# Four lists of rows per place, wide products first, and the odd groups' sums in the first four places: one change to a kernel of Fourier mixing and routed experts

## The chip, the cores and the metric

The kernel runs on one core of a Trainium2 chip. The metric is the device time of one execution in microseconds. Before the change it is 681.73 us, the median of three runs (681.48 to 681.78).

## The reference

2048 tokens of 512 numbers are normalised. Two things are added to them: a Fourier mixing, with the transform written as matrix products over the 512 columns and over the 2048 tokens, and a layer of eight experts, of which each token uses the one with the highest logit.

```python
def _A_ref(x, dft_seq_re, dft_seq_im, dft_hid_re, dft_hid_im):
    a = jnp.einsum("bsd,ed->bse", x, dft_hid_re)
    b = jnp.einsum("bsd,ed->bse", x, dft_hid_im)
    return jnp.einsum("ts,bse->bte", dft_seq_re, a) - jnp.einsum("ts,bse->bte", dft_seq_im, b)

def _B_ref(x, w_gate, w1, w2):          # S, D, F, E = 2048, 512, 1376, 8; K = 1
    logits = xf @ w_gate
    topk_idx = jnp.argsort(-logits, axis=-1)[:, :K]
    ...
    for e in range(E):
        mask = (topk_idx == e)
        w = (gates * mask).sum(-1, keepdims=True)
        h = _silu(xf @ w1[e]) @ w2[e]
        out = out + w * h

xn = _layernorm(x, axis=-1)
return x + _A_ref(xn, ...) + _B_ref(xn, ...)
```

## The kernel before

Every operand of a large product is held as a pair, a high part that ScalarE casts and a low part that VectorE subtracts (`split`, L126 and L127), and each product is three matmuls: high by high, high by low, low by high.

The work runs in this order. First the norms, and a product of the Fourier part with the sequence matrix (L412). Then its "even" groups (L598 to L600), beside which the gate's logits are counted, each expert's tokens are ranked, and every token's row is scattered to its place in a DRAM buffer. Then the experts. Then the "odd" groups of the Fourier part (again L598 to L600), and at last the product with the hidden matrices (L1228 to L1230), to which each token's expert row is added.

The experts are sorted by their number of tokens and each gets a *place*, the fullest first. The place's number of rows is fixed in the program. `SIZES` holds lists of eight such numbers; the program has an arm for each list, written out in full by `finish` (L1041), and a switch takes the first list that holds all the experts' counts. The table `less` holds the lists on the chip but the last; `set_apart` makes a spare tile of `APART` columns ahead of the experts' tiles.

A place is a `Window`. Its rows are loaded turned by a transposing DMA, joined to 32-bit numbers and split into a pair (`turns`), the tile `wth` (in the code `xx`). Then for each of 11 blocks of the hidden width (ten of 128, one of 96): `up` multiplies the place's rows by four chunks of the first weight matrix, silu follows on ScalarE, the result is split into `hh` (L930) and `hl` (L931), and two blocks later `down` multiplies it by the second weight matrix. The weights stream in through SyncE's queue, and their pairs are made three blocks ahead.

The two kinds of place differ in what stands still. With more than 256 rows, the weights are the stationary operand in both products and the moving one has as many columns as the place has rows: 12 matmuls up (L914 to L916) and 12 down (L954 to L956) for each block. With 256 rows or fewer (`twin`), the low part of the rows lies right behind the high part, so that one up matmul of twice the width multiplies both by the weights' high part (wide, 512 columns), and a narrow one multiplies the high part by the weights' low part; both are L911, and wide and narrow alternate over the four chunks, the last two swapped. The halves of the wide result are added by ScalarE and VectorE (L921, L922). Down, the rows are the stationary operand and the moving one has 512 columns: six matmuls (L946 to L948).

Beside the places, VectorE prepares the tokens' sums that the odd groups need, for one of eight token blocks in each place: at block 2 `odd_parts` adds the pair up (L515) and makes three sums (L518, L519), at block 5 `parts` casts and splits these (L498 on ScalarE, L499 on VectorE). All engines' instructions are put in order by a scheduler from the code's order and its own costs, save those that are pinned by `keep_in_program_order` and all of SyncE's.

Of the kernel before, what the change touches and what calls it, by code (L numbers as in the profile page):

```python
# [23 lines left out]
NB = NT // 2  # L24
KD = D // P
# [4 lines left out]
LAG = 2  # L30
RAWS = 4
PAIRS = 4
APART = 104
SHIFT = 56
WARM = 25
DH = D // 2
# [3 lines left out]

SIZES = [[300, 284, 276, 264, 256, 256, 256, 256],
         [310, 290, 278, 272, 266, 256, 256, 256],
         [328, 304, 288, 280, 270, 256, 256, 256]]
WS = SIZES[-1]
XW = 256
WCUM = [sum(WS[:i]) for i in range(E + 1)]
NX = max((S - sum(WS[:m]) + m * (XW - 1)) // XW for m in range(1, E + 1) if sum(WS[:m]) + m <= S)
assert min(map(min, SIZES)) > P and max(WS) <= 3 * P  # L50
assert all(a <= b for s in SIZES for a, b in zip(s, WS))


@with_exitstack
def fnet_moe(ctx, tc, x, cr, ci, dr, di, wg, w1, w1r, w2, w2r, out):
    nc = tc.nc
    V, A, T, G, SY = nc.vector, nc.scalar, nc.tensor, nc.gpsimd, nc.sync
# [11 lines left out]
    def bank(name):  # L69
        if free:  # L70
            return free.pop(0)
        return psum.tile([P, 512], F32, tag="bank", name=name)
# [242 lines left out]
    with tc.high_priority(), tc.manual_schedule(engines={V.engine, A.engine}):  # L315
# [11 lines left out]
        n = norms[1]  # L327
# [22 lines left out]
        n = norms[2]  # L350
# [34 lines left out]
    for i in range(E):  # L385
        G.memset(wsz[:, i:i + 1], float(WS[i]))
        G.memset(wcm[:, i:i + 1], float(WCUM[i]))
    less = cst.tile([P, len(SIZES) - 1, E], F32, name="less")
    for n, sizes in enumerate(SIZES[:-1]):
        for i in range(E):  # L390
# [106 lines left out]
    def parts(b, dst, src):  # L497
        copy = A.copy(xh[b].rearrange("p j d -> p (j d)")[:, dst], src)  # L498
        V.tensor_sub(xl[b].rearrange("p j d -> p (j d)")[:, dst], src,  # L499
                     xh[b].rearrange("p j d -> p (j d)")[:, dst].bitcast(F32))  # L500
        return copy
# [10 lines left out]
    def odd_parts(b):  # L512

        r = others.take()
        tc.keep_in_program_order(V.tensor_add(r, *(v[b].rearrange("p j d -> p (j d)").bitcast(F32) for v in (xh, xl))))  # L515
        t = sums.take()
        t2 = r[:, DH:2 * DH]
        V.tensor_add(t[:, DH:2 * DH], r[:, :DH], t2)  # L518
        V.tensor_add(*(v[:, 2 * DH:].rearrange("p (h d) -> p h d", h=2) for v in (t, r)),  # L519
                     t2[:, None, :].to_broadcast([P, 2, DH]))  # L520
        return r, t
# [131 lines left out]
    def sm(name, shape, dt=F32):  # L653
        return late[0].tile([P] + shape, dt, name=name)
# [57 lines left out]
    def route(cnt):  # L712
# [28 lines left out]
        def by_place(name, v, dst=None):  # L741
            m = sm("m" + name, [E, E])
            r = sm("r" + name, [E]) if dst is None else dst
            V.tensor_mul(m, q, v[:, None, :].to_broadcast([P, E, E]))
            V.reduce_sum(r, m, axis=AX.X)
            return r
# [15 lines left out]
        by_place("snu", num, over)  # L762
        n = len(SIZES) - 1
        past, most, no = sm("past", [n, E]), sm("most", [n]), sm("no", [n])
# [95 lines left out]
    def set_apart(pool):  # L860
        apart = pool.tile([P, APART], F32, name="apart", bufs=1)
        G.memset(apart, 0.0)

    class Window:
# [36 lines left out]
        def up(self, f):  # L901
            m, w = FT[f], self.w
            hi, lo = self.block(0, f // 2, 3)
            t = bank("up")
            for k in range(KD):
                c = (f % 2) * 512 + k * m
                h, l = (self.xx[:, k, a:a + w] for a in (self.at_h, self.at_l))
                if self.twin:
                    work = [(hi, self.xx[:, k, :2 * w], 2 * w), (lo, h, w)]
                    for a, b, n in work if k < KD - 1 else work[::-1]:  # L910
                        T.matmul(t[:m, :n], a[:, c:c + m], b, start=(k == 0 and a is hi),  # L911
                                 stop=(k == KD - 1 and a is hi))
                    continue
                T.matmul(t[:m, :w], hi[:, c:c + m], h, start=(k == 0), stop=False)  # L914
                T.matmul(t[:m, :w], hi[:, c:c + m], l, start=False, stop=False)  # L915
                T.matmul(t[:m, :w], lo[:, c:c + m], h, start=False, stop=(k == KD - 1))  # L916
            if f % 2 or f == NF - 1:
                self.release(0, f // 2)
            s = self.pool.tile([P, self.most], F32, name="sil")
            if self.twin:  # L920
                A.copy(s[:m, :w], t[:m, w:2 * w])  # L921
                V.tensor_add(s[:m, :w], t[:m, :w], s[:m, :w])  # L922
                A.activation(s[:m, :w], s[:m, :w], AF.Silu)
            else:
                A.activation(s[:m, :w], t[:m, :w], AF.Silu)
            free.append(t)
            hh = self.pool.tile([P, self.most], F32R, name="hh", bufs=3)
            hl = self.pool.tile([P, self.most], F32R, name="hl", bufs=3)
            hh, hl = (v[:, self.at_h:self.at_h + w] for v in (hh, hl))
            (A.copy if self.twin and f % 2 else V.tensor_copy)(hh[:m], s[:m, :w])  # L930
            V.tensor_sub(hl[:m], s[:m, :w], hh[:m].bitcast(F32))  # L931
            self.pend.append((f, hh, hl))
# [108 lines left out]
    def finish(sizes, last):  # L1041
# [45 lines left out]
        for i, w in enumerate(wins):  # L1087
            for f in range(NF):
                w.up(f)
                todo.append(w)  # L1090
                if len(todo) > LAG:
                    todo.pop(0).down()
                if f == 2:
                    halves3 = odd_parts(i)
                if f == 5:
                    tc.keep_in_program_order(parts(i, slice(DH, 4 * DH), halves3[1][:, DH:]))
                    others.give(halves3[0])
                    sums.give(halves3[1])
                if i == 0 and f == 8:
                    more.append(mo.enter_context(tc.tile_pool(name="more", bufs=1)))  # L1100
                if i + 1 < E:
                    if f in (3, 4):
                        wins[i + 1].load(f - 3)
                    if f in (6, 8):
                        wins[i + 1].turns(f - 6)
                if i > 0:
                    w0 = wins[i - 1]
                    if w0.twin and f in (2, 3):
                        w0.back(f - 2)
                    if not w0.twin and 6 <= f < 9:  # L1110
                        w0.turn(f - 6)
                    if not w0.twin and f == 10:
                        w0.store()
# [135 lines left out]
        with tc.If(more_windows[0] > 0):  # L1249
            with tc.tile_pool(name="zeros", bufs=1) as zp:  # L1250
                zero = zp.tile([P, 2 * D], U16, name="zero")
                G.memset(zero, 0)
                n = NX * XW // P
                A.dma_start(hx[:n * P, :].rearrange("(n p) d -> p n d", p=P), zero[:, None, :].to_broadcast([P, n, 2 * D]))
                A.dma_start(hx[n * P:, :], zero[:1, :])
            with tc.For_i(0, more_windows[0]) as j, tc.tile_pool(name="further", bufs=1) as fp, \
# [7 lines left out]
                def block(k, b, ahead):  # L1264
                    if (k, b) not in got:
# [3 lines left out]
                w = Window(XW, lambda r, n: xs[bass.ds(xov + r, n), :],  # L1269
                           lambda r, n: hx[bass.ds(j * XW + r, n), :], block, fp)  # L1270
# [27 lines left out]
    for n in tc.Switch(which[0], len(SIZES), hint="sizes"):  # L1298
        finish(SIZES[n], n == len(SIZES) - 1)
# [44 lines left out]
```

## Time and profile before

| | us |
|---|---|
| median of the runs | 681.73 |
| the profiled execution | 681.63 |
| its span, first to last instruction | 679.9 |
| TensorE's matmuls busy | 673.6 |
| VectorE busy | 532.1 |
| ScalarE busy | 407.7 |
| GpSimd busy | 46.3 |

In the rows of the profile, PE is TensorE's matmuls and PEld its weight loads, DVE is VectorE, ACT ScalarE, POOL GpSimd, SP SyncE; a q behind a name is that engine's DMA queue. A row of the timeline has the start, the duration, the engine, the line, the operation, what is written and what is read, the shape (for a matmul rows and columns of the array, then the moving operand), and in brackets how long the engine was idle before and what ended that. Ends of matmuls are modelled, starts are recorded. The experts' places lie between 230.8 and 490 us: those of more than 256 rows, 300, 284, 276 and 264, begin at 230.8, 264.0, 298.7 and 332.2 us, the four of 256 fill the time from 364.1 us on.

### The profile page before, as it was taken

To read this page: it belongs to the slowest core of one execution; us is meant where nothing else is said; L and a number is where in the kernel's file an instruction comes from. 1 tells how busy PE (TensorE), PEld (TensorE's weight loads), DVE (VectorE), ACT (ScalarE), POOL (GpSimd) and SP (SyncE) were. 2 spreads that over 40 slices of the span, in tenths; PEclk is the share of its full clock that TensorE was granted. 3 is DMA by queue.
4 is the path that set the end of the run, shared out by engine and by line. 5 is a ranking of instruction groups with operands and counts; after the bars stand their busy time and mean duration, and the time that the engine had idled before them with its cause. 6 is when DMAs were issued, how large, how long until landed. Compare 5 with 4: busy or idle time off the path is not lost.

```text
span 679.9 us, 10515 instructions
## 1 busy us (share of the span) xinstructions
PE 673.6 (99%) x3635; PEld 578.0 (85%) x3635; DVE 532.1 (78%) x908; ACT 407.7 (60%) x666; POOL 46.3 (7%) x84
## 2 busy tenths in 40 slices
PE   8999999999999999999999999999999999999997
PEld 6788867888888899999999888888888888888886
DVE  6897367998968586868687988989977889696841
ACT  5766255755856656666667787787635566463430
POOL 2000000602210000000000000000020000031200
PEclk9999999999999999999999999999999999999999
DMA  9644385898976856989767985846686898897931
GB/s 302 229 155 119 129 316 195 287 346 285 318 234 225 278 167 213 218 260 224 251 182 255 250 259 189 244 160 236 214 283 221 293 314 276 297 351 292 321 110 65
DMA packets 81278, 162.52 MB, mean 239 GB/s; under 512 B 36284, under 2 KB 37564, under 8 KB 81217
## 3 DMA queue, kind: packets, MB, share of 16 engines
q1 hardware_dynamic: 71231, 133.33, 61.3%
q10 hardware_dynamic: 7426, 20.06, 7.7%
q0 software_dynamic: 2560, 8.39, 3.5%
q8 instruction: 30, 0.49, 0.3%
q14 instruction: 31, 0.25, 0.1%
HBM read 127.47 MB, written 26.68 MB: 227 GB/s over the span
## 4 chain that ended last, share of the span: by engine, by line
PE 97%; DVE 1%; ACT 1%; DMA 0%; issue 0%; DVEq 0%
PE s L598 11%; PE s L600 11%; PE s L599 11%; PE acc L412 11%; PE s L911 9%; PE s L1229 4%; PE s L1230 4%; PE s L1228 4%; PE s L914 3%; PE s L954 3%; PE s L956 3%; PE s L916 3%; PE s L955 3%; PE s L915 3%; PE s L946 3%; PE s L948 3%
## 5 line engine op out<-in xcount | busy, mean ns | idle before, releaser
L127 DVE TENSOR_TENSOR lo<-raw,hi 128x1024 fp32r<-128x1024 f32 (+2 forms) x115 | 130.2, 1136 | 40.8 <-ACT hi L126 39.6
L126 ACT CAST hi<-raw 128x1024 fp32r<-128x1024 f32 (+2 forms) x115 | 112.7, 985 | 45.0 <-PE s L915 20.2
L599 PE MATMUL s<-lo,xh 128*128 128x512 f32 x336 | 130.9, 389 | 0.0
L600 PE MATMUL s<-hi,xl 128*128 128x512 f32 x336 | 130.8, 389 | 0.0
L598 PE MATMUL s<-hi,xh 128*128 128x512 f32 x336 | 130.2, 390 | 0.0
L526 ACT CAST hi<-sums 128x1024 fp32r<-128x1024 f32 x48 | 50.4, 1050 | 63.1 <-PE s L600 34.8
L598 PEld LDWEIGHTS s<-hi,xh 128*128 128x128 f32 x336 | 63.1, 188 | 14.7 <-ACT sp L430 0.8
L599 PEld LDWEIGHTS s<-lo,xh 128*128 128x128 f32 x336 | 63.1, 188 | 13.5 <-DVE lo L530 0.4
L600 PEld LDWEIGHTS s<-hi,xl 128*128 128x128 f32 x336 | 63.1, 188 | 13.0
L530 DVE TENSOR_TENSOR lo<-sums,hi 128x1024 fp32r<-128x1024 f32 x48 | 58.6, 1221 | 16.4 <-ACT hi L526 16.4
L911 PE MATMUL s<-wth,hi 128*128 128x512 f32 (+1 forms) x176 | 64.6, 396 | 0.0
L914 PE MATMUL s<-wth,hi 128*128 128x300 f32 (+7 forms) x176 | 51.3, 292 | 0.0
L915 PE MATMUL s<-wth,hi 128*128 128x300 f32 (+7 forms) x176 | 51.3, 291 | 0.0
L955 PE MATMUL s<-hl,hi 128*128 128x300 f32 (+7 forms) x176 | 51.2, 291 | 0.0
L956 PE MATMUL s<-hh,lo 128*128 128x300 f32 (+7 forms) x176 | 51.2, 291 | 0.0
L916 PE MATMUL s<-wth,lo 128*128 128x300 f32 (+7 forms) x176 | 51.1, 291 | 0.0
L954 PE MATMUL s<-hh,hi 128*128 128x300 f32 (+7 forms) x176 | 50.8, 291 | 0.0
L412 PE MATMUL acc<-hi,xh 128*128 128x512 f32 x128 | 49.4, 390 | 0.7 <-DVE xh L260 0.7
L412 PE MATMUL acc<-lo,xh 128*128 128x512 f32 x128 | 49.3, 389 | 0.0
L412 PE MATMUL acc<-hi,xl 128*128 128x512 f32 x128 | 48.8, 391 | 0.1
L526 ACT CAST hi<-raw 128x512 fp32r<-128x512 f32 (+1 forms) x44 | 36.0, 817 | 13.9 <-PE s L600 11.2
L530 DVE TENSOR_TENSOR lo<-raw,hi 128x512 fp32r<-128x512 f32 (+1 forms) x44 | 40.8, 927 | 3.5 <-ACT hi L526 3.4
(242 smaller groups left out, 1418.3 us busy)
## 6 DMA issues: line engine op xcount, KB each, us to landing
raw<-in_w SPq DMA_DIRECT2D x80, 512.0 KB
raw<-in_ci SPq DMA_DIRECT2D x36, 512.0 KB
raw<-in_cr SPq DMA_DIRECT2D x30, 512.0 KB
other<-in_ci SPq DMA_DIRECT2D x16, 512.0 KB
p<-sp ACTq DMA_DIRECT2D x12, 512.0 KB
q<-sp ACTq DMA_DIRECT2D x9, 512.0 KB
other<-p SPq DMA_DIRECT2D x9, 512.0 KB
other<-in_cr SPq DMA_DIRECT2D x8, 512.0 KB
```

The source lines that it names most:

```text
L126: A.copy(hi, raw)
L127: V.tensor_sub(lo, raw, hi.bitcast(F32))
L412: T.matmul(acc[k], x_[b][:, j, k * P:(k + 1) * P], c_, start=(s == 0 and x_ is xh and c_ is ch), stop=(s == NT - 1 and x_ is xl))
L526: A.copy(hi[:, :n], t[:, cols])
L530: V.tensor_sub(lo[:, :n], t[:, cols], hi[:, :n].bitcast(F32))
L598: T.matmul(acc[name][k], a, ch, start=(b == 0), stop=False)
L599: T.matmul(acc[name][k], a, cl, start=False, stop=False)
L600: T.matmul(acc[name][k], al, ch, start=False, stop=(b == NB - 1))
L911: T.matmul(t[:m, :n], a[:, c:c + m], b, start=(k == 0 and a is hi), stop=(k == KD - 1 and a is hi))
L914: T.matmul(t[:m, :w], hi[:, c:c + m], h, start=(k == 0), stop=False)
L915: T.matmul(t[:m, :w], hi[:, c:c + m], l, start=False, stop=False)
L955: T.matmul(y, hi[:m, c:c + P], hl[:m], start=False, stop=False)
```

## The change

There are four lists in place of three, and rows under 256 are among them. In a place of 256 or fewer rows, all four wide up products come first, then the four narrow ones. The sums for the odd groups are made in the first four places only, two token blocks in each: at blocks 1 and 4, and at 6 and 9. The spare tile loses 8 columns, as many as the longer table `less` takes ahead of it.

```diff
-APART = 104
+APART = 96
...
-SIZES = [[300, 284, 276, 264, 256, 256, 256, 256],
-         [310, 290, 278, 272, 266, 256, 256, 256],
-         [328, 304, 288, 280, 270, 256, 256, 256]]
+SIZES = [[294, 280, 272, 264, 256, 256, 254, 250],
+         [300, 284, 274, 268, 264, 256, 252, 238],
+         [316, 294, 282, 274, 256, 252, 246, 244],
+         [328, 302, 288, 276, 268, 264, 256, 250]]
...
             t = bank("up")
-            for k in range(KD):
+            if self.twin:
+                for v, n in ((hi, 2 * w), (lo, w)):
+                    for k in range(KD):
+                        c = (f % 2) * 512 + k * m
+                        T.matmul(t[:m, :n], v[:, c:c + m], self.xx[:, k, :n], start=(k == 0 and v is hi),
+                                 stop=(k == KD - 1 and v is lo))
+            for k in () if self.twin else range(KD):
                 c = (f % 2) * 512 + k * m
                 h, l = (self.xx[:, k, a:a + w] for a in (self.at_h, self.at_l))
-                if self.twin:
-                    work = [(hi, self.xx[:, k, :2 * w], 2 * w), (lo, h, w)]
-                    for a, b, n in work if k < KD - 1 else work[::-1]:
-                        T.matmul(t[:m, :n], a[:, c:c + m], b, start=(k == 0 and a is hi),
-                                 stop=(k == KD - 1 and a is hi))
-                    continue
...
-                if f == 2:
-                    halves3 = odd_parts(i)
-                if f == 5:
-                    tc.keep_in_program_order(parts(i, slice(DH, 4 * DH), halves3[1][:, DH:]))
+                if f in (1, 6) and 2 * i < NB:
+                    halves3 = odd_parts(2 * i + f // 6)
+                if f in (4, 9) and 2 * i < NB:
+                    tc.keep_in_program_order(parts(2 * i + f // 9, slice(DH, 4 * DH), halves3[1][:, DH:]))
```

The lines behind this part stand one line lower in the changed kernel. How the order moves shows at three places. The first is TensorE in the first place of 256, from its fifth block on; `s` with a number is a PSUM bank, `wth` the place's rows, `hi` and `lo` a pair of weights. Before:

```order
L911 MATMUL s_2168<-wth,lo 128x256
L911 MATMUL s_2168<-wth,hi 128x512
L911 MATMUL s_2168<-wth,lo 128x256
L911 MATMUL s_2168<-wth,hi 128x512
L911 MATMUL s_2168<-wth,lo 128x256 x2
L911 MATMUL s_2168<-wth,hi 128x512
L911 MATMUL s_2169<-wth,hi 128x512
L946 MATMUL s_2153<-hi,hh 128x512
L947 MATMUL s_2153<-lo,hh 128x512
L948 MATMUL s_2153<-hi,hl 128x512
```

Here a block's up products end, the scheduler has drawn the first wide product of the next block ahead, and the products down follow. In the changed kernel the same place reads:

```order
L910 MATMUL s_2178<-wth,hi 128x512 x4
L910 MATMUL s_2178<-wth,lo 128x256 x4
L947 MATMUL s_2162<-hi,hh 128x512
L948 MATMUL s_2162<-lo,hh 128x512
L949 MATMUL s_2162<-hi,hl 128x512
L947 MATMUL s_2169<-hi,hh 128x512
L948 MATMUL s_2169<-lo,hh 128x512
L949 MATMUL s_2169<-hi,hl 128x512
```

The wide and the narrow ones stand in two runs, and no block is broken by another. The second place is VectorE early in the second place of rows (284 before, 280 now), where it also copies the last place's result out (`yw`); `xh` and `xl` are the tokens' pair, `other` and `sums` hold the sums. Before:

```order
L127 TENSOR_TENSOR lo<-raw,hi 128x1024
L961 COPY yw<-s_2168 128x2x128
L930 CAST hh<-sil 128x284
L931 TENSOR_TENSOR hl<-sil,hh 128x284
L515 TENSOR_TENSOR other<-xh_99,xl_107 128x1024
L518 TENSOR_TENSOR sums<-other 128x256
L519 TENSOR_TENSOR sums<-other 128x512
L930 CAST hh<-sil 128x284
L127 TENSOR_TENSOR lo<-raw,hi 128x1024
L931 TENSOR_TENSOR hl<-sil,hh 128x284
```

And now:

```order
L128 TENSOR_TENSOR lo<-raw,hi 128x1024
L962 COPY yw<-s_2177 128x2x128
L516 TENSOR_TENSOR other<-xh_100,xl_108 128x1024
L931 CAST hh<-sil 128x280
L519 TENSOR_TENSOR sums<-other 128x256
L520 TENSOR_TENSOR sums<-other 128x512
L932 TENSOR_TENSOR hl<-sil,hh 128x280
L931 CAST hh<-sil 128x280
L128 TENSOR_TENSOR lo<-raw,hi 128x1024
L932 TENSOR_TENSOR hl<-sil,hh 128x280
```

The sums now stand ahead of the hh and hl of the second block, not behind them, and those of another token block follow later in the same place. The third is VectorE in the first place of 256. Before:

```order
L127 TENSOR_TENSOR lo<-raw,hi 128x1024
L930 CAST hh<-sil 128x256
L931 TENSOR_TENSOR hl<-sil,hh 128x256
L515 TENSOR_TENSOR other<-xh_102,xl_110 128x1024
L931 TENSOR_TENSOR hl<-sil,hh 128x256
L518 TENSOR_TENSOR sums<-other 128x256
L519 TENSOR_TENSOR sums<-other 128x512
L127 TENSOR_TENSOR lo<-raw,hi 128x1024
```

And now:

```order
L923 TENSOR_TENSOR sil<-s_2161,sil 128x256
L128 TENSOR_TENSOR lo<-raw,hi 128x1024
L931 CAST hh<-sil 128x256
L923 TENSOR_TENSOR sil<-s_2170,sil 128x256
L932 TENSOR_TENSOR hl<-sil,hh 128x256
L128 TENSOR_TENSOR lo<-raw,hi 128x1024
L932 TENSOR_TENSOR hl<-sil,hh 128x256
```

No sums are left there: silu's input (`sil`), the weights' low parts, hh and hl follow each other.

## The prediction

> **What bounds the kernel now.** I read the page first, then two stretches of the table by windows, then the timeline of TensorE. From the page, the span, TensorE's busy row, and the chain of work that ended last, by engine:
>
> ```profile
> span 679.9 us, 10515 instructions
> PE 673.6 (99%) x3635; PEld 578.0 (85%) x3635; DVE 532.1 (78%) x908; ACT 407.7 (60%) x666; POOL 46.3 (7%) x84
> PE 97%; DVE 1%; ACT 1%; DMA 0%; issue 0%; DVEq 0%
> ```
>
> The chain is TensorE from end to end. So what the change takes from TensorE's sequence shortens the run one for one, and work on another engine counts only where TensorE waits for it. A busy share says little about matmuls, whose ends are modelled; what I price is the pitch, the time from one matmul's start to the next one's. Now the experts' part, the four places of more than 256 rows and then the four of 256 (windows; the columns are the stretch, its length, busy time of each engine, the granted clock, the share of DMA, GB/s):
>
> ```profile
> 230.80:364.10 133.30, 133.30 (x1034) 133.30 (x1033) 101.43 (x171) 85.25 (x159) 0.00 (x0) 1.00 0.78 231
> 364.10:491.00 126.90, 126.90 (x647) 105.99 (x646) 113.44 (x202) 98.14 (x199) 0.00 (x0) 1.00 0.72 221
> ```
>
> TensorE never rests, the clock is whole, VectorE works 76% of the first stretch and 89% of the second. The change lies within these two stretches, 260 us of the span. Now the pitch by width, from starts in TensorE's timeline that lie twelve products apart (300, 284, 276, 264 columns, and 256 in the kernel's last part):
>
> ```profile
> 262.34 0.30 PE L954 MATMUL s<-hh,hi 128*128 128x300 f32 x1
> ...
> 264.00 0.30 PE L914 MATMUL s<-wth,hi 128*128 128x284 f32 x1
> ...
> 265.57 0.30 PE L954 MATMUL s<-hh,hi 128*128 128x300 f32 x1
> ...
> 298.69 0.29 PE L914 MATMUL s<-wth,hi 128*128 128x276 f32 x1
> ...
> 300.21 0.29 PE L954 MATMUL s<-hh,hi 128*128 128x284 f32 x1
> ...
> 332.24 0.28 PE L914 MATMUL s<-wth,hi 128*128 128x264 f32 x1
> ...
> 333.68 0.29 PE L954 MATMUL s<-hh,hi 128*128 128x276 f32 x1
> ...
> 661.42 0.28 PE L1228 MATMUL s<-dh,hi 128*128 128x256 f32 x1
> ...
> 662.86 0.28 PE L1228 MATMUL s<-dh,hi 128*128 128x256 f32 x1
> ```
>
> 1.66 us for twelve products of 300 columns are 138 ns each; 1.57 us are 131 ns at 284, 1.52 us are 127 ns at 276, 1.44 us are 120 ns at 264, and 1.44 us again 120 ns at 256. The last pair matters: from 264 to 256 nothing is gained.
>
> **Narrower rows in the first four places.** The list that this run takes is the first (the trace has 300, 284, 276, 264); the reference's draw, worked through its layer norm and gate, gives counts of 293, 279, 263, 260, 247, 242, 232, 232, so the new first list holds them too: 294, 280, 272, 264, 256, 256, 254, 250. A place of this kind has 11 row blocks of 4 x 3 products up and 4 x 3 down, 264 in all, each as wide as the place. Reading straight lines between the pitches above, 294 comes to 135.4 ns, 280 to 129 and 272 to 124.5: together about 7 ns less, times 264, 1.9 us. But the four pitches also fit steps of 8 columns, 3.4 ns each (264 is 33 steps, 276 begins its 35th, 284 its 36th, 300 its 38th); then 294 has 37 steps, 280 has 35 and 272 has 34, which saves 4.3, 4 and 3.4 ns, 3.1 us in all. The rows do not decide between the two; I take 2.3 us, nearer to the straight lines, which need no rule. The lower bound is under the rivals.
>
> **The order of an up product.** The next rows are one row block of a place of 256: four wide products (both parts of the tokens against the high part of the weights, 512 columns) and four narrow ones, then six of 512 down to the next block (TensorE's timeline; x2 joins two of a kind):
>
> ```profile
> 372.55 0.39 PE L911 MATMUL s<-wth,hi 128*128 128x512 f32 x1
> 372.77 0.28 PE L911 MATMUL s<-wth,lo 128*128 128x256 f32 x1
> 372.88 0.40 PE L911 MATMUL s<-wth,hi 128*128 128x512 f32 x1
> 373.12 0.28 PE L911 MATMUL s<-wth,lo 128*128 128x256 f32 x1
> 373.24 0.40 PE L911 MATMUL s<-wth,hi 128*128 128x512 f32 x1
> 373.48 0.40 PE L911 MATMUL s<-wth,lo 128*128 128x256 f32 x2
> 373.71 0.40 PE L911 MATMUL s<-wth,hi 128*128 128x512 f32 x1
> 373.95 0.40 PE L946 MATMUL s<-hi,hh 128*128 128x512 f32 x1
> 374.19 0.39 PE L947 MATMUL s<-lo,hh 128*128 128x512 f32 x1
> ...
> 375.32 0.39 PE L911 MATMUL s<-wth,hi 128*128 128x512 f32 x1
> ```
>
> From 374.19 to 375.32 five wide products follow wide ones: 226 ns each. Among the mixed ones a wide product takes 220 ns once and then 240, 240 and 240, a narrow one 110 to 120, and the first one down 240. The block takes 2.77 us; wide after wide and narrow after narrow would be 10 x 0.226 + 4 x 0.120 = 2.74 us. At the 10 ns of these rows that is 20 to 30 ns a block; I take 25 ns, times 44 blocks: 1.1 us. Bounds: nothing, if the slow wide products have another cause, and 2.0 us if the narrow ones keep their 110 ns. The products, their operands and their number stay.
>
> **Rows under 256.** The last two places shrink to 254 and 250: (2 + 6) x 3 columns x 4 x 11 = 1056 columns. Between 300 and 512 columns the rows give (226 - 138) / 212 = 0.41 ns a column, so 0.4 us at most; if the narrow products stay at 120 ns, as between 264 and 256, the wide two thirds are left: 0.3 us, which I take; the least is 0. The products down keep 512 columns. The last two places now write their rows by two DMAs in place of one from ScalarE's queue; nobody reads them before the end, so I cost that at nothing. So with the fourth arm of the switch, the eight table entries more that GpSimd, 7% busy, writes at the start, and the spare tile of 96 columns in place of 104: the table grows by 8 columns ahead of it, so the experts' tiles stay where they are.
>
> **Waits of TensorE in the places of 256.** The first and the last of six such spots, on TensorE, and what VectorE does at the first:
>
> ```profile
> 376.49 0.63 PE L911 MATMUL s<-wth,hi 128*128 128x512 f32 x2
> 377.05 0.50 PE L946 MATMUL s<-hi,hh 128*128 128x512 f32 x1
> 377.38 0.40 PE L947 MATMUL s<-lo,hh 128*128 128x512 f32 x1
> ...
> 474.43 0.63 PE L911 MATMUL s<-wth,hi 128*128 128x512 f32 x2
> 474.93 0.50 PE L946 MATMUL s<-hi,hh 128*128 128x512 f32 x1
> 475.26 0.39 PE L947 MATMUL s<-lo,hh 128*128 128x512 f32 x1
> ```
>
> ```profile
> 375.56 1.22 DVE L127 TENSOR_TENSOR lo<-raw,hi 128x1024 fp32r<-128x1024 f32 x1 [0.43 <-ACT hi L126]
> 376.70 0.29 DVE L930 CAST hh<-sil 128x256 fp32r<-128x256 f32 x1
> ```
>
> Three wide products should take 0.68 us; they take 0.89 and 0.83. At the first spot the product down starts when VectorE has cast its hh, which stood behind a split of weights. Over the six spots (near 376.7, 395.7, 408.0, 438.3, 457.1 and 474.7) the starts lie 0.8 us too far apart in sum. The change takes the sums for the odd groups out of these places, and its program for TensorE is whole again there, eight up, six down, where the first spot had a piece of the next block drawn ahead. I take 0.6 us; between 0 and 0.8.
>
> **What the moved sums cost.** One set of sums, from the groups by line over the experts' part (count, busy us, mean ns), and how long TensorE leaves VectorE for a row block's low part in the second place (end of hl, and its first use):
>
> ```profile
> L515 DVE TENSOR_TENSOR other<-xh,xl 128x1024 f32<-128x1024 f32 x8 | 9.8, 1219 | 0.0
> L499 DVE TENSOR_TENSOR xl<-sums,xh 128x768 fp32r<-128x768 f32 x8 | 7.6, 950 | 0.0
> L519 DVE TENSOR_TENSOR sums<-other 128x512 f32<-128x512 f32 x8 | 5.5, 685 | 0.0
> L518 DVE TENSOR_TENSOR sums<-other 128x256 f32<-128x256 f32 x8 | 3.4, 419 | 0.1
> ```
>
> ```profile
> 271.61 0.45 DVE L931 TENSOR_TENSOR hl<-sil,hh 128x284 fp32r<-128x284 f32 x1
> ...
> 275.30 0.29 PE L955 MATMUL s<-hl,hi 128*128 128x284 f32 x1
> ```
>
> A set is 3.3 us of VectorE: a run of 2.3 us and later 0.95 us. The first four places get four sets more, 13 us, and VectorE comes to (101.4 + 13.1) / 133.3 = 86% there; the last four are relieved of as much. In the new order a run of 2.3 us stands ahead of that hl, whose slack is 3.2 us: 0.9 us are left. So I expect cover, with small misses: 0.3 us, between 0 and 2. ScalarE's part of a set (the cast at L498) has 36% of idle time about it.
>
> **The sum.** 2.3 + 1.1 + 0.3 + 0.6 - 0.3 = 4.0 us off the span of 679.9 us: 675.9 us. The profiled execution took 681.63 us with what lies around its span; 677.6 us follows. The median of the runs before, 681.73 us, is 0.1 us above that execution: 677.7 us. About 0.2%, 1.4 us, is what a measurement of this kernel can tell from no change.
>
> **Rivals.** First, *only columns count*: a column costs 0.41 ns at any width, and the order of wide and narrow nothing, the slow wide products being due to something that stays. Then the first four places give 14 x 0.41 x 264 = 1.5 us, the last two 0.4, the order 0, the waits 0.6, the sums -0.3: 2.2 us, 679.5 us. For it speaks that 300 and 512 lie on that line; against it, that 264 to 300 costs 0.5 ns a column, and how evenly the slow wide products follow narrow ones. The Trainium skill has it so in TensorE: Matmul & The Clock Gate, section Back-to-back issue gap: columns over 2.4 plus 2.5 ns, at whole clock. By that page 512 and 256 columns would take 216 and 109 ns in either order, so the order would be worth nothing; the trace's 226 and 120 ns do not agree with it.
>
> Second, *the moved sums hold TensorE up*, and the kernel is slower. Place: the run ahead of hl in the second row block of each of the first four places, where VectorE also copies the last place's result out. It decides where the slack falls under the run, 2.3 us. With two weight splits of 1.22 us (the row at 375.56) drawn ahead of it as well, hl would come 2.3 + 2.4 - 3.2 = 1.5 us late; at all four places 6 us, and 4.3 us off elsewhere: 1.7 us slower, 683.4 us. Against it: those splits have their own slack, and today's run stands in the same place without a wait on TensorE.
>
> Third, *the new list doesn't hold*: if the chip counts otherwise, the second list runs (300, 284, 274, 268, 264, 256, 252, 238). The fifth place would then have 264 products of 120 ns, 31.7 us, where 11 blocks of 2.77 us are 30.5: +1.2 us. The fourth pays 4 columns, +0.6, the third saves 0.3; the last three places save 33 x 25 ns = 0.8 in order and 0.8 in wide columns, waits 0.5; with the sums' 0.3 it is 0.3 us off, 681.4 us.
>
> **Chances and range.** The forecast 0.74, only columns 0.17, the sums 0.05, the other list 0.04. The forecast's own range goes from 676.3 (3.1 + 1.1 + 0.4 + 0.8 off, the sums hidden) to 679.0 (1.9 off by straight lines, order and waits worth half, 0.3 for the rows and -0.3 for the sums). To hold 8 in 10 it takes in the first rival: 676.2 to 680.0. Faster by over 0.2% is under 680.4: nearly all of the first two cases, 0.89; within 0.2%: 0.06; slower: 0.05.
>
> **What would show it.** In the profile after: twelve products of 294, 280 and 272 columns in 1.62, 1.54 and 1.49 us; a row block of a place of 256 in 2.74 us, with wide starts 226 to 227 ns and narrow ones 120 ns apart; fewer spots where three wide products take over 0.75 us; no start in the first four places later than its neighbours by over 0.2 us. I am wrong if a block of 256 still takes 2.77 us, if the narrower widths save under 1.5 us, or if waits for hl appear beside the moved sums.

## The result, and the profile after

The changed kernel takes 689.89 us, the median of five runs (688.62 to 690.62), where the kernel before takes 681.73 us beside it (681.48 to 681.93): a ratio of 1.0121, 95% interval 1.0110 to 1.0131. It is 8.2 us slower, and the forecast was 4.0 us faster. The span, TensorE's busy row and the chain by engine, from the page after:

```profile
span 688.0 us, 10540 instructions
PE 677.2 (98%) x3635; PEld 578.9 (84%) x3635; DVE 533.0 (77%) x909; ACT 407.8 (59%) x666; POOL 49.1 (7%) x92
PE 87%; DVE 5%; ACT 4%; issue 2%; DMA 2%; SPq 0%; ACTq 0%; DVEq 0%
```

The chain is no longer TensorE's alone: VectorE and ScalarE have 9% of it together. Where that is, the windows tell; the first two rows are one answer, for the four places of more than 256 rows and the four of 256 or fewer, the others a second answer, for four pieces of the latter (columns as before):

```profile
230.80:362.50 131.70, 131.70 (x1034) 131.53 (x1033) 110.27 (x186) 88.32 (x163) 0.00 (x0) 1.00 0.80 234
362.50:496.50 134.00, 128.26 (x643) 105.73 (x642) 104.99 (x187) 95.10 (x195) 0.00 (x0) 0.99 0.69 211
```

```profile
370.00:400.00 30.00, 30.00 (x154) 25.37 (x152) 24.72 (x45) 24.45 (x52) 0.00 (x0) 1.00 0.87 256
400.00:430.00 30.00, 30.00 (x153) 25.29 (x152) 23.61 (x43) 22.50 (x47) 0.00 (x0) 1.00 0.78 210
430.00:460.00 30.00, 28.32 (x140) 22.79 (x139) 22.49 (x41) 21.34 (x43) 0.00 (x0) 1.00 0.60 196
460.00:500.00 40.00, 35.94 (x160) 28.11 (x159) 28.86 (x53) 22.20 (x44) 0.00 (x0) 0.93 0.56 195
```

The first stretch takes 131.7 us where it took 133.3, without a gap, though VectorE has the moved sums there (84% busy; 86% was forecast). The second takes 134.0 us, where the places of 256 filled 126 us (364.1 to 490 us): 8 us longer. In it TensorE is busy without a gap from 370 to 430 and has gaps from 430 on, in the places of 254 and 250 rows; and there VectorE and ScalarE are less busy, not more (22.5 and 21.3 us from 430 to 460, where the kernel before has 27.2 and 24.2). No engine is overloaded: the engines wait for each other. The granted clock falls as well, to 0.93 in the last piece. TensorE's waits over the whole run (line waited for, us in total, times, longest):

```profile
PE s L947 <- DVE hh L931: 2.4, 2, 2.2
PE s L949 <- DVE hl L932: 1.5, 3, 0.7
PE s L910 <- ACT hi L127: 1.3, 1, 1.3
```

None of these stood in the same answer for the kernel before. They make 5.2 us. What follows the longest, on TensorE:

```profile
491.06 0.40 PE L949 MATMUL s<-hi,hl 128*122 128x512 f32 x1
493.69 0.50 PE L947 MATMUL s<-hi,hh 96*128 96x512 f32 x1 [2.24 <-DVE hh L931]
...
495.21 0.63 PE L947 MATMUL s<-hi,hh 96*122 96x512 f32 x1
495.64 0.63 PE L948 MATMUL s<-lo,hh 96*122 96x512 f32 x1
...
500.33 0.63 PE L599 MATMUL s<-hi,xh 128*128 128x512 f32 x1
500.76 0.52 PE L600 MATMUL s<-lo,xh 128*128 128x512 f32 x1
```

After the wait the starts lie 427 ns apart, not 227, from 495.2 to 500.8 us: TensorE runs at half its clock, and these 13 products lose 2.6 us more.

What the forecast said of widths and order can be read here too. TensorE's starts twelve products apart, at 294 and 280 columns, and one block of a place of 256 up to the next one's first products (x4 joins four of a kind):

```profile
230.78 0.30 PE L915 MATMUL s<-wth,hi 128*128 128x294 f32 x1
...
232.39 0.30 PE L915 MATMUL s<-wth,hi 128*128 128x294 f32 x1
...
262.81 0.29 PE L915 MATMUL s<-wth,hi 128*128 128x280 f32 x1
...
264.35 0.30 PE L955 MATMUL s<-hh,hi 128*128 128x294 f32 x1
...
373.70 1.07 PE L910 MATMUL s<-wth,hi 128*128 128x512 f32 x4
374.60 0.64 PE L910 MATMUL s<-wth,lo 128*128 128x256 f32 x4
375.08 0.40 PE L947 MATMUL s<-hi,hh 128*128 128x512 f32 x1
...
376.46 1.07 PE L910 MATMUL s<-wth,hi 128*128 128x512 f32 x4
```

1.61 us for twelve of 294 columns are 134 ns each, 1.54 us 128 ns at 280. In the block, four wide products take 0.90 us (225 ns each) and four narrow ones 0.48 (120 ns): the slow starts are gone from the up products, as forecast. But the six down then take 1.38 us, 230 ns each, and the block 2.76 us instead of 2.77: most of the slowness has moved behind the narrow ones and not gone.

### The profile page after: what moved, and what is told of

Same layout as the page of the kernel before. It is cut to its first block, busy times and chain, and to the rows that moved or that the text cites. A ratio compares the mean times of both kernels' runs of the same rounds, so it can differ in the third digit from the quotient of the medians.

```text
span 688.0 us, 10540 instructions
## 1 busy us (share of the span) xinstructions
PE 677.2 (98%) x3635; PEld 578.9 (84%) x3635; DVE 533.0 (77%) x909; ACT 407.8 (59%) x666; POOL 49.1 (7%) x92
## 4 chain that ended last, share of the span: by engine, by line
PE 87%; DVE 5%; ACT 4%; issue 2%; DMA 2%; SPq 0%; ACTq 0%; DVEq 0%
PE s L599 11%; PE s L600 11%; PE s L601 11%; PE acc L413 11%; PE s L910 5%; PE s L1231 4%; PE s L1230 4%; PE s L1229 4%; PE s L917 3%; PE s L956 3%; PE s L916 3%; PE s L957 3%; PE s L915 3%; PE s L955 3%; PE s L949 2%
## 5 line engine op out<-in xcount | busy, mean ns | idle before, releaser
L127 ACT CAST hi<-raw 128x1024 fp32r<-128x1024 f32 (+2 forms) x115 | 111.9, 984 | 42.0 <-PE s L916 15.3
L601 PE MATMUL s<-hi,xl 128*128 128x512 f32 x336 | 131.5, 391 | 0.0
L916 PE MATMUL s<-wth,hi 128*128 128x294 f32 (+7 forms) x176 | 51.0, 290 | 0.0
L956 PE MATMUL s<-hl,hi 128*128 128x294 f32 (+7 forms) x176 | 51.0, 290 | 0.0
L917 PE MATMUL s<-wth,lo 128*128 128x294 f32 (+7 forms) x176 | 50.9, 290 | 0.0
L957 PE MATMUL s<-hh,lo 128*128 128x294 f32 (+7 forms) x176 | 50.9, 290 | 0.0
L915 PE MATMUL s<-wth,hi 128*128 128x294 f32 (+7 forms) x176 | 50.8, 289 | 0.0
L955 PE MATMUL s<-hh,hi 128*128 128x294 f32 (+7 forms) x176 | 50.4, 289 | 0.0
L910 PE MATMUL s<-wth,hi 128*128 128x512 f32 (+5 forms) x176 | 47.4, 391 | 1.3 <-ACT hi L127 1.3
```

The costliest lines, as they stand in the source:

```text
L127: A.copy(hi, raw)
L601: T.matmul(acc[name][k], al, ch, start=False, stop=(b == NB - 1))
L910: T.matmul(t[:m, :n], v[:, c:c + m], self.xx[:, k, :n], start=(k == 0 and v is hi), stop=(k == KD - 1 and v is lo))
L956: T.matmul(y, hi[:m, c:c + P], hl[:m], start=False, stop=False)
```

## The experiments

My theory was that the rows under 256 bring the loss; the rivals were the other parts of the change, each by itself. Ratios are against runs of the kernel before on the same chip, which took 681.5 to 681.8 us; brackets hold the 95% interval.

**One part undone.** rows256 takes the rows under 256 out of the list that runs.

```diff
-SIZES = [[294, 280, 272, 264, 256, 256, 254, 250],
+SIZES = [[294, 280, 272, 264, 256, 256, 256, 256],
```

> The change with its first list ended by 256, 256 in place of 254, 250 (and 256 for 250 at the end of the last list, which does not run). Theory one, rows under 256 bring the waits of TensorE from 430 to 495 us: those go, about 11 us with the half clock after them, and the time is about 678.5 us. Theory two, the moved sums bring them, and theory three, wide products first bring them: about 689.5 us, within 1 us of the change.

Measured: 678.87 us, 0.9963 [0.9949, 0.9977]. Eight rows fewer, two in one place and six in another, turn 2.6 us of gain into 8.2 us of loss: 10.8 us. With the other parts kept, the run beats the kernel before.

old_sums puts the sums back to one token block in each of eight places, old_up the alternating order of the up products:

```diff
-                if f in (1, 6) and 2 * i < NB:
-                    halves3 = odd_parts(2 * i + f // 6)
...
+                if f == 2:
+                    halves3 = odd_parts(i)
+                if f == 5:
...
```

```diff
-            if self.twin:
-                for v, n in ((hi, 2 * w), (lo, w)):
-                    for k in range(KD):
...
+            for k in range(KD):
...
+                if self.twin:
+                    work = [(hi, self.xx[:, k, :2 * w], 2 * w), (lo, h, w)]
+                    for a, b, n in work if k < KD - 1 else work[::-1]:
...
```

> The change with the odd groups' sums back at one set in each place, blocks 2 and 5. Theory one (rows under 256): the waits in the last two places stay, 688 to 691 us. Theory two (moved sums): they go, about 679 us. Theory three (wide first): 688 to 691 us.

Measured: 692.88 us, 1.0175 [1.0156, 1.0194]: not the sums. With the rows under 256 kept, the time is over 3 us longer than the change's, more than either theory said: there the sums are better where the change has them.

> The change with wide and narrow up products alternating as before. Theory one (rows under 256 alone): the waits stay, 688 to 691 us. Theory three (wide products first, or these together with rows under 256): the waits shrink, 679 to 681 us. Theory two (moved sums): 688 to 691 us.

Measured: 686.26 us, 1.0074 [1.0049, 1.0099]: below the 688 to 691 us that the first theory gave. Most of the loss stays, so the order of the up products is not its cause, but with the old order it is some 3 us smaller.

**One part alone**, in the kernel before. lists_only has the new lists (and `APART = 96`), widths_only the new list with its last two places at 256, up_only wide before narrow, sums_only the moved sums.

> The kernel before with the new lists (and the spare tile of 96 columns) alone: order of products and sums as before. Theory one in its strict form, rows under 256 alone bring the waits: 688 to 690 us. If it takes wide first or moved sums as well: the narrower rows give their 1.9 us, rows under 256 cost up to 0.5, and the time is about 680 us.

Measured: 689.08 us, 1.0117 [1.0100, 1.0133]: the lists alone bring the whole loss, with the old order of the up products and the old sums.

> The kernel before with the first list at 294, 280, 272, 264 and four times 256, products and sums in the order of before. Narrower rows alone: 1.9 us off by the pitches of the changed kernel (133.4, 129.7, 125.4 and 120 ns at 294, 280, 272 and 264), so 679.6 us; by the steps of 8 columns 678.4.

Measured: 679.91 us, 0.9974 [0.9965, 0.9984]: 1.7 us off, near the 1.9 us of the straight lines between the pitches; the steps of 8 columns, 3.1 us, lie outside the interval.

> The kernel before with the wide up products first, lists and sums as before. By the changed kernel's blocks (1380 + 1387 ns in place of 1406 + 1367 up and down) the order itself gives 6 ns a block, 0.3 us; the six waits of 0.8 us may go with the unbroken order: 680.6 us. By my prediction, 25 ns a block and 0.6 us: 680.0.

Measured: 680.47 us, 0.9981 [0.9972, 0.9990]: 1.2 us off.

> The kernel before with the odd groups' sums moved to the first four places, lists and products as before. If the sums in the places of 256 caused the six waits: 0.6 us less, 681.0 us; if they cost waits in the first four places: 682 us; if neither, 681.6 us.

Measured: 681.95 us, 1.0005 [0.9996, 1.0014]: 0.3 us, not to be told from nothing.

**What of the rows under 256.** pad256 keeps 254 and 250 rows, but gives the rows a room of 256, so that the up products there have 512 and 256 columns again. two_stores is rows256 with two stores for each of the last two places, as 254 and 250 rows have. narrow_only is rows256 with only the narrow up product of the last two places cut to 254 and 250 columns, so that it leaves two and six columns of one of the three products out; narrow_four does the same in all four places of 256, with 254.

```diff
-            self.at_l = rows if self.twin else self.most + SHIFT
+            self.mw = 256 if self.twin else rows
+            self.at_l = self.mw if self.twin else self.most + SHIFT
...
-            w = self.w
+            w = self.mw
...
-                for v, n in ((hi, 2 * w), (lo, w)):
+                for v, n in ((hi, 2 * self.mw), (lo, self.mw)):
...
-                A.copy(s[:m, :w], t[:m, w:2 * w])
+                A.copy(s[:m, :w], t[:m, self.mw:self.mw + w])
```

```diff
-            if j == 1 and n == P:
+            if j == 1 and n == P and not self.apart:
```

```diff
-                for v, n in ((hi, 2 * w), (lo, w)):
+                for v, n in ((hi, 2 * w), (lo, w - self.less)):
...
+        wins[6].less, wins[7].less = (2, 6) if wins[6].twin else (0, 0)
```

> The change with rows of 254 and 250 kept in the last two places, but their up products over 256 and 512 columns (the columns beyond the rows are other tokens' and are dropped before silu). Theory A, the scheduler prices a narrow product of fewer than 256 columns so that it puts VectorE's and ScalarE's work too late: the order is then that of the run with 256 rows, the waits go, 679 us. Theory B, rows under 256 themselves cost the chip time (odd widths, 126 and 122 stationary columns, two stores a place): 687 to 690 us.

Measured: 679.29 us, 0.9967 [0.9954, 0.9979]: the rows themselves, with the additions, silus and splits that VectorE and ScalarE do on 254 and 250 columns, cost nothing that this run shows.

> The run with 256 rows in the last four places, but the last two write their rows by two DMAs in place of one, as places under 256 do. Theory B in the form that ScalarE's queue waits in the second DMA for VectorE: 680 us and more. Theory A: 678.9 us, within 0.5.

Measured: 678.91 us, 0.9960 [0.9946, 0.9974]: nor do the stores.

> The run with 256 rows in the last four places, but the narrow up products of the last two take 254 and 250 of the 256 columns (the rows left out of this one product, the last 2 and 6 of a place, hold no token of that expert in this draw). Nothing else differs. Theory A (the scheduler's price of a product under 256 columns): the waits come back, 686 to 690 us. Theory B (the rows elsewhere): 678.9 us, within 0.5.

Measured: 689.80 us, 1.0123 [1.0106, 1.0140]: 88 products that are two or six columns shorter bring the whole loss (8.2 us above the kernel before, where rows256 is 2.6 us below).

> The run with 256 rows in the last four places, with a narrow product of 254 columns in all four of them. If the scheduler's price of a product under 256 columns puts the work late in each place where it stands: waits in places five and six too, twice the loss of two places or so, 695 to 705 us. If only the last place (its handover to the odd groups) is weak: 690 us.

Measured: 694.27 us, 1.0180 [1.0165, 1.0196]: more places, more loss, but less than twice: 15.2 us against rows256, where two places bring 10.8 us.

So the place was found, and the result made no sense by columns: in narrow_only's trace from these 88 products to the next start it is 110 to 121 ns, save for five, as with 256. Two causes were left. The chip could finish such a product late; or the order, in which the scheduler puts ScalarE's and VectorE's instructions, could be another where a product has fewer than 256 columns. TensorE's own order differs from that of rows256 in one pair of products. The trace of the change had the cast of the next place's first weights late on ScalarE, so casts_first moved these casts forward, in the last two places:

```diff
-            ready[k] = (loaded.pop(k) if k in loaded else load())()
+            get = loaded.pop(k) if k in loaded else load()
+            if k[0] == "w" and k[1] > 5:
+                with tc.high_priority():
+                    ready[k] = get()
+            else:
+                ready[k] = get()
```

> The change, rows of 254 and 250 and their narrow products kept, but the scheduler is told to put the weights' casts and splits of the last two places as early as it can. If the late order is what costs, most of the 11 us of waits and half clock go: 679 to 682 us. If products under 256 columns cost the chip time by themselves: 688 us or more.

Measured: 688.04 us, 1.0089 [1.0073, 1.0104]. A miss: 2 us came back, where most of the 11 us were expected. Read by what was expected, this spoke for the chip being slow with such products; the next pair shows otherwise. The edit moved little: in the program of casts_first ScalarE still has the silu straight behind the copy before it in 15 of the 22 blocks of the last two places, in that of the change in 17 (what that means is told below).

**Order or columns.** The pair that decides takes the two apart. cut_254 is rows256, put in order with 256 columns; then the finished programs are changed, and the narrow products of the last two places cut to 254 and 250 columns. fill_256 is narrow_only, put in order with 254 and 250, its narrow products then widened to 256. after_cut is the change itself, treated as cut_254: all its sums are whole.

```diff
     with tile.TileContext(nc) as tc:
         fnet_moe(tc, *args)
+    cut(nc)
...
+    def short(a, n):
+        return copy.replace(a, ap=[list(q) for q in a.ap[:-1]] + [[1, n]], bass_ap=None)
...
+                program[j] = copy.replace(v, outs=[short(v.outs[0], n)], ins=[short(v.ins[0], n), v.ins[1]])
```

> Four lists with 256 rows in all the last four places, as in rows256, and every engine's program in rows256's order, instruction for instruction; only the narrow up products of the last two places are cut to 254 and 250 columns after the order has been made (as in narrow_only, their other columns are left out of the sums). If narrow_only's 689.8 us came from the order that the scheduler makes of ScalarE and VectorE when a product has fewer than 256 columns, this is rows256's 678.9 us less 88 products by 1 to 3 ns: 678.4 to 679.1, with no waits of TensorE in the last two places. If the chip itself is slow with products under 256 columns (a late end of the product, a slower read of its bank), it is about 689.8, with the waits for hh, hl and hi back.

Measured: 678.67 us, 0.9958 [0.9941, 0.9974].

> The other half of the pair: narrow_only with every engine's program in narrow_only's order, but the narrow up products of the last two places widened back to 256 columns after the order has been made; no column is left out now. If the order is the cause: 689.5 to 690.2 us, with narrow_only's waits (hh 2.6 us, hi 1.6, hl 1.5) although no product has fewer than 256 columns. If the columns are the cause: 678.9 us and no waits.

Measured: 690.57 us, 1.0134 [1.0117, 1.0151].

> The change with its own rows (254 and 250 in the last two places), but ordered as if the narrow up products there had 256 columns, and cut to 254 and 250 after that. If the order is the whole loss: the 689.9 us of the change less its 11 us, that is rows256's 678.9 less what the six fewer rows save, 44 products of 504 to 508 columns for 512 and 44 of 250 to 254 for 256 in each place at 0.42 ns a column (0.3 us): 678.4 to 679.1. If rows under 256 cost something on the chip beside the order: 680 to 690.

Measured: 678.93 us, 0.9958 [0.9942, 0.9975]. The change has eight rows fewer than rows256, not six, and its wide products have 508 and 500 columns, so columns alone would save 0.4 us here and not 0.3; these runs don't tell the two apart.

The three answers agree. TensorE's waits in fill_256, whose products in these places all have 256 columns or more, are those of narrow_only and of the change (its lines stand one lower):

```profile
PE s L948 <- DVE hh L932: 2.6, 2, 2.3
PE s L950 <- DVE hl L933: 1.9, 4, 0.9
PE s L911 <- ACT hi L127: 1.6, 1, 1.6
```

In cut_254, with 254 and 250 columns, TensorE waits for nothing but the warm-up at the start:

```profile
PE spare L273 <- DVE eps L276: 1.1, 1, 1.1
```

The loss goes with the order and not with the columns; in these runs a product of 254 columns costs the chip nothing more than one of 256 (cut_254 0.9958, rows256 0.9963).

**What the order does.** Here the program of the change (+) stands against that of after_cut (-), on ScalarE in the middle of the place of 254, from its fifth to its seventh block. L922 copies the low half of the wide result out of PSUM, VectorE adds it to the other half (L923), L924 is the silu of that sum, L931 a cast to hh, L127 a cast of weights:

```
 L922 COPY sil<-s_2153 128x254
-L127 CAST hi<-raw 128x1024
 L924 ACTIVATE sil<-sil 128x254
+L127 CAST hi<-raw 128x1024
 L922 COPY sil<-s_2154 128x254
 L127 CAST hi<-raw 128x1024
-L127 CAST hi<-raw 128x384
 L924 ACTIVATE sil<-sil 128x254
+L127 CAST hi<-raw 128x384
+L931 CAST hh<-sil 128x254
 L922 COPY sil<-s_2162 128x254
-L931 CAST hh<-sil 128x254
-L127 CAST hi<-raw 96x512
 L924 ACTIVATE sil<-sil 128x254
```

In after_cut a cast stands between a copy and its silu; in the change the silu comes first and the cast behind it. In the last two places a silu stands straight behind the copy of its own block for 6 of the 22 blocks in after_cut's program and for 17 in the change's; for 7 in rows256 and for 17 in fill_256. ScalarE then has nothing to do until VectorE has added. In the trace of the change, and at the same work in that of after_cut (ScalarE's timeline, the tenth block of the same place):

```profile
453.15 0.36 ACT L922 COPY sil<-s 128x254 f32<-128x254 f32 x1
454.33 0.42 ACT L924 ACTIVATE sil<-sil 128x254 f32<-128x254 f32 x1 [0.82 <-DVE sil L923]
454.78 0.40 ACT L931 CAST hh<-sil 128x254 fp32r<-128x254 f32 x1
455.09 1.04 ACT L127 CAST hi<-raw 128x1024 fp32r<-128x1024 f32 x1
```

```profile
451.76 0.35 ACT L922 COPY sil<-s 128x254 f32<-128x254 f32 x1
452.07 2.01 ACT L127 CAST hi<-raw 128x1024 fp32r<-128x1024 f32 x2
453.98 0.42 ACT L924 ACTIVATE sil<-sil 128x254 f32<-128x254 f32 x1
```

In after_cut two casts fill the time of VectorE's addition, and the silu finds its sum ready. In the change ScalarE stands for 0.82 us and does the casts afterwards. ScalarE's waits for that sum from 400 to 500 us, in the change, in after_cut, and in the pair fill_256 and cut_254:

```profile
ACT sil L924 <- DVE sil L923: 27.9, 27, 2.8
```

```profile
ACT sil L924 <- DVE sil L923: 11.8, 15, 1.4
```

```profile
ACT sil L925 <- DVE sil L924: 28.3, 27, 2.9
```

```profile
ACT sil L924 <- DVE sil L923: 12.0, 15, 1.4
```

after_cut and cut_254 bear 12 us of such idle time without a wait of TensorE; with 28 us ScalarE falls behind. The silu of the last block of the sixth, seventh and eighth place, in the change and in after_cut:

```profile
425.45 0.42 ACT L924 ACTIVATE sil<-sil 96x256 f32<-96x256 f32 x1 [1.59 <-DVE sil L923]
458.88 0.42 ACT L924 ACTIVATE sil<-sil 96x254 f32<-96x254 f32 x1 [1.54 <-DVE sil L923]
492.87 0.41 ACT L924 ACTIVATE sil<-sil 96x250 f32<-96x250 f32 x1 [1.56 <-DVE sil L923]
```

```profile
425.95 0.42 ACT L924 ACTIVATE sil<-sil 96x256 f32<-96x256 f32 x1
456.50 0.41 ACT L924 ACTIVATE sil<-sil 96x254 f32<-96x254 f32 x1
485.46 0.41 ACT L924 ACTIVATE sil<-sil 96x250 f32<-96x250 f32 x1 [0.83 <-DVE sil L923]
```

A place takes ScalarE 33.4 and 34.0 us in the change, and 30.6 and 29.0 us in after_cut: 7.9 us more over the two. The 30.6 us are TensorE's pace (a place of 256 takes 11 blocks of 2.77 us, 30.5 us). TensorE loses as much. Its two programs differ in one pair of products, so the starts of the others can be set side by side. At 430.67 us the change is 0.5 us ahead of after_cut, which starts the same product at 431.18 us. The products that start at 493.69 us, after the long wait, and at 500.76 us, at the end of the half clock (both are shown above), start in after_cut at:

```profile
486.47 0.40 PE L947 MATMUL s<-hi,hh 96*128 96x512 f32 x1
...
490.33 0.39 PE L600 MATMUL s<-lo,xh 128*128 128x512 f32 x1
```

The change is 7.2 us behind at the first and 10.4 us at the second. So 7.7 us are lost up to the end of the long wait, and 3.2 us behind it: 10.9 us together. In casts_first ScalarE still waits for the sum 23 times and 25.5 us (in the profiled execution, which at 690.15 us was the slowest of its four); that fits the little that it gave.

The place of the casts is not all of it. ScalarE's longest wait for the sum, 2.83 us before the silu at 477.05 us, holds a wait of VectorE for a DMA. In the change VectorE has one of the sums for the odd groups (L577) ahead of that block's addition (L923), and its input has not landed:

```profile
476.00 0.69 DVE L577 TENSOR_TENSOR sums<-raw 128x512 f32<-128x512 f32 x1 [2.19 <-DMA raw<-in_ci]
476.61 0.41 DVE L923 TENSOR_TENSOR sil<-s,sil 128x250 f32<-128x250 f32 x1
```

In after_cut the additions of this block and of the next come first, and the same sum waits for nothing:

```profile
471.82 0.41 DVE L923 TENSOR_TENSOR sil<-s,sil 128x250 f32<-128x250 f32 x1
...
474.02 0.41 DVE L923 TENSOR_TENSOR sil<-s,sil 128x250 f32<-128x250 f32 x1
474.35 0.68 DVE L577 TENSOR_TENSOR sums<-raw 128x512 f32<-128x512 f32 x1
```

The DMA was also issued later, at 472.32 us against 468.64 us. VectorE has such a wait, 2.1 to 2.4 us long, in the trace of every run that loses, and in none of the others. And in lists_only, with the old order of the up products, a silu stands straight behind its copy in only 9 of the 22 blocks, and ScalarE waits 23.2 us for the sum all the same. How much the order of ScalarE weighs, and how much that of VectorE, no run separates.

That the order is the cause is shown by the pair. That it works through the copy, the addition and the silu is read from the traces and not shown: no run moved only those rows. Why the scheduler makes another order under 256 columns is not shown by any run: it puts the engines in order by its own costs, and a narrow product that is dearer in them would do it.

## Why the prediction was wrong, point by point

- **What bounds the kernel: right for before, and left too early.** TensorE's chain of 97% was that of the kernel before. How closely ScalarE and VectorE wait for each other in the places of 256 was not priced. VectorE's 89% there was read, but the busy share is not what failed: the loss came with VectorE 75% and 72% busy, from 430 to 460 and from 460 to 500 us.
- **Rows under 256: the step that failed.** It said 0.3 us gained, "the least is 0", and priced the two places by their columns and their stores alone. By columns it was right as far as the runs can tell: cut_254 and after_cut stand at 0.9958 of before, rows256 at 0.9963, and their intervals overlap. What was not priced is that the scheduler orders the whole of the two places anew, and not for TensorE: I compared TensorE's order in a place of 256 ("its program for TensorE is whole again") and VectorE's in two places, and looked at no engine in the two places whose shapes change. That cost about 11 us: 10.8 by rows256 against the change, 11.1 by after_cut against the change, 11.9 by cut_254 against fill_256.
- **Narrower rows in the first four places: too large by 0.5 us.** 2.3 us were taken; widths_only has 1.7 us by its times (1.1 to 2.4 by the interval), and in its trace the four places take 131.5 us instead of 133.3: 1.8 us. The straight lines (1.9) were right, the steps of 8 columns are out.
- **The order of an up product: too large by 0.8 us.** 25 ns a block were taken, 1.1 us. The median block takes 2.774 us in the trace of the kernel before and 2.767 us in that of up_only: 7 ns, 0.3 us over 44 blocks. The wide products are at 225 ns, but the down products behind the narrow ones rose to 230 ns.
- **The waits beside it: nearly right, for one of its two reasons.** 0.6 us was taken. up_only has 1.2 us for order and waits together, which leaves 0.9 us for the waits; its trace has no spot left where three wide products take over 0.75 us. sums_only, from whose places of 256 the sums are gone, still has such spots (0.84 us from 444.00 us on). So the waits went with the unbroken order and not with the sums. That the two terms, 1.7 us, come as near to 1.2 us as they do is in part luck: one was too large, the other too small.
- **The moved sums: right as far as can be told.** 0.3 us was taken, between 0 and 2. By its times sums_only has 0.3, which can't be told from nothing; in its trace the first four places take 133.5 us instead of 133.3. No wait of TensorE in these places names the sums.
- **The sum without the failed step** would have been 1.7 + 1.2 - 0.3 = 2.6 us off, with the sizes that the single parts showed. rows256 has 2.6 us, after_cut 2.9.
- **The rivals and the signs.** No rival was it. The slower one, with a chance of 0.05, had the right kind of mechanism, VectorE late for TensorE, in the wrong places and from the wrong part of the change. Of the signs of being wrong that it names, the first, a block that still takes 2.77 us, all but came up (2.767 us), and it points at the order of the products and not at the loss; no sign was set on the last two places alone, where the loss lay. The list that ran was the first, as worked out: the trace has 294, 280, 272, 264, 256, 256, 254 and 250 rows.

## What to carry to other kernels

Where a scheduler orders the engines, a shape can change the order of every engine, and not only the number of columns on one: compare before and after on all engines in each stage whose shapes change, and above all on those that feed the bound engine with little to spare. If an edit of a few columns moves microseconds, keep the order and change the columns, then keep the columns and change the order; that pair told in two runs what the twelve before it had only located. As the traces read here, a round trip between two engines (copy, add, silu) needs other work placed into it on the engine that waits, and nothing ahead of its step on the other; an order that gives this up can make the trip the pace of the stage without any engine being busier.

## What the runs showed of the hardware

In the change a pause of 2.6 us between two starts (491.06 to 493.69 us) was followed by half clock: starts 427 ns apart for 512 columns from 495.2 to 500.8 us, with this granted clock (third figure from the right):

```profile
495.00:500.00 5.00, 5.00 (x13) 3.86 (x13) 2.05 (x4) 1.69 (x3) 0.00 (x0) 0.50 0.59 210
```

So this wait cost 2.4 us itself (the pause less one pitch) and 3.2 us behind it. The length of a pause alone does not tell whether this happens. In old_sums TensorE paused 2.76 us, from 456.11 to 458.87 us, and the clock stayed whole:

```profile
456.00:464.00 8.00, 5.54 (x28) 4.09 (x27) 6.57 (x12) 4.73 (x10) 0.00 (x0) 1.00 0.36 120
```

In the same run a shorter pause, 2.26 us before the start at 487.81 us, was followed by starts 427 ns apart. What decides is not shown.

Narrow products among wide ones make a block longer than its pitches alone: ten wide ones of 226 ns and four narrow ones of 120 ns would be 2.74 us. The median block takes 2.774 us with the two kinds mixed (the kernel before) and 2.767 us with each kind in one run (up_only): the order moved the extra time to the products behind, and took 7 ns off it.
